# Block-causal attention ahead of two feed-forward layers on one core: every PSUM bank a tile of its own, attention's steps and copies cut by head and bank

## The chip, the cores and the metric

One core of a Trainium2 chip runs the whole program. The metric is device microseconds (us) of one execution, the median of 3 runs. The engines are named as the profile names them: PE is TensorE (PEld its weight load), DVE is VectorE, ACT is ScalarE, POOL is GpSimd, SP is SyncE, which here only starts DMAs. PSUM is the memory that TensorE writes; it has 8 banks of 512 fp32 for each of 128 partitions, and in this kernel DVE and ACT read the products from it.

## The reference, cut to what matters

```python
# q, k, v: (4, 8, 576, 64) fp32; x: 2304 tokens x 512; both layers 512 -> 2048 -> 512
scores = scale * np.matmul(q, k.transpose(0, 1, 3, 2))
mask = (pos[:, None] // 64) >= (pos[None, :] // 64)
scores = np.where(mask, scores, -1e9)
scores = scores - np.max(scores, axis=-1, keepdims=True)
attn = np.exp(scores)
attn = attn / (np.sum(attn, axis=-1, keepdims=True) + 1e-9)
x = np.matmul(attn, v)            # heads side by side: 2304 x 512
h = x @ w_in;  x = np.maximum(h, 0) ** 2 @ w_out
h = x @ w_in2; y = (h * np.cos(h)) @ w_out2
```

## The kernel before

The 32 heads of 576 tokens are taken as 16 pairs (p = 0 to 15), two heads (e = 0, 1) in each. Queries come in five row blocks: m = 0 to 3 of 128 queries each, which see 128(m+1) keys, and the last 64 queries, which see all 576. The last queries of two neighbouring pairs (Q = p // 2) share one step, since 2 x 64 queries fill the 128 partitions. `attention()` does all of it before `layers()` does the two feed-forward layers, whose matmuls (lines 727 and 794) split each fp32 factor into a high and a low half.

For each pair there are these steps, and the line that the profile shows for each:

- **load** (395, 396, 413): keys `kB`, queries `qB` and values `vB` by DMA; **k scale** (400) on GpSimd. Pair 0's keys and queries come in two parts, 256 and 320 keys.
- **scores** (427): a matmul for each head and half block into `ps`. One PSUM tile is a double, `[128, 2, 512]`: head 0 in its first bank, head 1 in its second. There are four doubles.
- **maximum** (475, DVE) and **exponential** (481, ACT, with the row sums in `sums`): one for each head, from PSUM into `P`.
- **last** (454, then 475 and 481 as well): the last 64 queries of two pairs, into two doubles; head e takes one double, the two halves of the keys its two banks. One maximum and one exponential over all 576 keys for each head, into `PL`.
- **guard** (502, GpSimd, adds 1e-9), **invert** (507, DVE), **scale** (519 GpSimd, 517 ACT): divides the rows.
- **turn** (558) and **turn last** (583): transposes of 128x128 on TensorE into a double, both heads in one step. **turned** (564) and **turned last** (597): copies from the double to `PT`, both heads in one instruction of up to 768 elements, on ACT or DVE.
- **weighted** (616): `PT` times values, into one bank, `holds=1`; two for each pair, the first 256 queries and the other 320. **keep** (625) copies that bank to `xall`.

The order is not written out. Every step is added to a `Plan` with its engine, an assumed cost, its reads and writes, the number of banks that it holds and a rank (`RANK`, three numbers for each kind of step). `Plan.emit` then walks a clock of its own over the engines, takes at each turn the step that can start first (of those the one of lowest rank), chooses its banks (`room`) and emits it. Each engine runs its instructions in the order of emission. The waits between engines come from the framework, which looks at the accesses to a tile: one that follows another engine's in the order of emission waits for it. It does so by tile, and a double is one tile.

`weights`, `shift`, `mask` and their like (257 to 310) prepare the layers' weights; `cut` (351, 354) splits `xall` for the first layer. Both begin inside attention.

Of the kernel before, what the change touches and what calls it, by code (L numbers as in the profile page):

```python
# [28 lines left out]
    "load": (-1070.1, 12335.9, 3315.9),  # L29
    "k scale": (4499.4, 4439.0, 10407.1),  # L30
    "scores": (-3717.3, -3706.2, -4224.4),
    "maximum": (-4123.2, -5928.6, -2791.5),
    "exponential": (-2882.2, -4488.5, -2823.0),
    "last": (-4277.4, 3387.7, 5215.9),
    "maximum last": (4504.6, -3957.5, 2890.3),
    "exponential last": (5026.5, 8137.9, 3199.7),
    "guard": (-7573.3, 98.1, 5585.7),
    "invert": (-370.9, -1350.6, 1118.4),
    "scale": (8255.0, 13810.4, 13542.6),
    "guard last": (11229.8, 12038.7, 351.1),  # L40
    "invert last": (-2810.2, -7044.6, -10537.8),
    "scale last": (-6927.0, -1451.2, -1971.5),
    "turn": (9961.4, 12162.8, 5856.4),
    "turned": (-8239.7, -3277.3, -4164.1),
    "turn last": (-7032.9, -15612.2, -19327.9),
    "turned last": (1967.2, -1490.1, -1385.7),
    "value load": (-254.9, -122.1, 2369.7),
    "weighted": (9996.3, 12685.1, 17820.3),
    "keep": (11719.5, 11790.9, 1623.7),
    "weights": (12395.5, 9732.3, 12201.5),  # L50
# [4 lines left out]
class Plan:  # L55
# [8 lines left out]
    STAY = 0.087  # L64

    def __init__(self, doubles):
        self.doubles = doubles
        self.steps, self.wrote, self.readers = [], {}, {}
        self.taken, self.due = {}, {}
# [22 lines left out]
    def bank(self, n, x=0):  # L92
        b = self.taken[n][x]
        return self.doubles[b // 2][:, b % 2]

    def double(self, n, x=0):
        return self.doubles[self.taken[n][2 * x] // 2]

    def room(self, free, holds, t=None):

        if holds == 1:
            able = [(max(at - (t or 0.0), 0.0) if t is not None else at, b ^ 1 in free, b) for b, at in free.items()]
            if not able:
                return None
            b = min(able)[2]
            return free[b], [b]
        pairs = sorted((max(free[b], free[b + 1]), b) for b in free if not b % 2 and b + 1 in free)
        if 2 * len(pairs) < holds:
            return None
        pairs = pairs[: holds // 2]  # L110
        return pairs[-1][0], [b + x for _, b in pairs for x in range(2)]

    def emit(self):
# [13 lines left out]
        free = {b: 0.0 for b in range(2 * len(self.doubles))}  # L127
# [58 lines left out]
def tile_block_causal_attention__then__two_ffn(  # L186
# [174 lines left out]
    def attention():  # L361
        with ExitStack() as actx:
            ap = actx.enter_context(tc.tile_pool(name="ap", bufs=1))
            ps = actx.enter_context(tc.tile_pool(name="ps", bufs=1, space=PSUM))
            plan = Plan([ps.tile([128, 2, 512], F32, name=f"ps{r}") for r in range(4)])
# [7 lines left out]
            PT = [ap.tile([128, NCH, 2, S], F32, name=f"PT{r}") for r in range(2)]  # L373
# [4 lines left out]
            def small(name, n, r):  # L378
                return ap.tile([128, n], F32, name=f"{name}{r}")

            nmax = [[[small(f"nmax{m}.{e}.", 1, r) for e in range(2)] for m in range(NCH)] for r in range(2)]
            sums = [[small(f"sums{g}.", 2 * len(ms), r) for g, ms in enumerate([*groups, (4,)])] for r in range(2)]
            rinv = [[small(f"rinv{g}.", 2 * len(ms), r) for g, ms in enumerate([*groups, (4,)])] for r in range(2)]

            def add_loads(p):
                r, x = p // 2 % 2, p % 2

                cuts = [0, 4, NB] if p == 0 else [0, NB]
                parts = list(zip(cuts, cuts[1:]))
                other = nc.scalar if p == 0 else nc.sync  # L390
                for n, (b0, b1) in enumerate(parts):
                    keys = [f"{y}{r}.{x}.{z}" for y in "kq" for z in (range(2) if p else (n,))]

                    def load(b0=b0, b1=b1):
                        nc.sync.dma_start(out=kB[r][:, x, b0 * D : b1 * D], in_=kT[p, :, b0 * D : b1 * D])
                        other.dma_start(out=qB[r][:, x, b0:b1], in_=qd[p, :, b0:b1])

                    def scale(b0=b0, b1=b1):
# [6 lines left out]
                        "D", (2.8 if p else 2.9 if n == 0 else 1.2), ("load", 10 * p + n), load, writes=keys  # L405
# [3 lines left out]
                        writes=[y for y in keys if y[0] == "k"],  # L409
# [7 lines left out]
            def add_scores(p, m):  # L417
# [4 lines left out]
                def product():  # L422
                    held = plan.double(s)
                    for e, own in enumerate(heads):
                        for h, half in enumerate(heads):
                            c, w = n - 128 + h * D, n - D + h * D
                            nc.tensor.matmul(  # L427
                                held[half, e, 512 - n : 512 - n + w], lhsT=qB[r][own, x, c // D, e],
                                rhs=kB[r][own, x, 0:w], start=True, stop=True,
                            )  # L430
# [3 lines left out]
                    [f"{y}{r}.{x}.{z}" for y in "kq" for z in range(1 if m < 2 else 2)], [f"S{p}.{m}", f"free{x}.{m}"],  # L434
# [4 lines left out]
                add_softmax(  # L439
                    p, x, m, s, f"S{p}.{m}", rank, g, at,  # L440
                    lambda e: plan.double(s)[:, e, 512 - n : 512],
                    lambda e: P[x][:, p_off[m] + e * n :][:, 0:n], n,
                )

            def add_last(Q):

                r, w = Q % 2, S // 2
                rank = 20 * Q

                def product():  # L450
                    for y in range(2):
                        for e, own in enumerate(heads):
                            for x, half in enumerate(heads):
                                nc.tensor.matmul(
                                    plan.double(s, e)[half, y, 0:w], lhsT=qB[r][own, x, NB - 1, e],
# [3 lines left out]
                keys = [f"{a}{r}.{x}.{z}" for a in "qk" for x in range(2) for z in range(2)]  # L459
                s = plan.add(  # L460
                    "P", 4 * S / 2400, ("last", rank), product, keys, [f"SL{Q}", f"free{r}.L"],
                    holds=4, mode="quarters", late=0.4,
                )
                add_softmax(
                    Q, r, NCH - 1, s, f"SL{Q}", rank, len(groups), 0,
                    lambda e: plan.double(s, e)[:, :, 0:w],
                    lambda e: PL[r][:, e, 0:S].rearrange("p (y w) -> p y w", y=2), S,
                )

            def add_softmax(p, r, m, s, at, rank, g, c, held, mine, n):  # L470
                one = m < NM
                name = m if one else "L"

                def maximum(e):
                    nc.vector.tensor_reduce(
                        out=nmax[r][m][e], in_=held(e), axis=AX.X if one else AX.XY,
                        op=ALU.max, negate=True,
                    )

                def exponential(e):  # L480
                    nc.scalar.activation(  # L481
                        out=mine(e), in_=held(e), func=AF.Exp, bias=nmax[r][m][e], scale=1.0,
                        accum_out=sums[r][g][:, c + e : c + e + 1],
                    )

                for e in range(2):
                    kind = "" if one else " last"
                    plan.add(
# [466 lines left out]
```

## Time and profile before

| | us |
|---|---|
| median of 3 runs | 971.17 (971.08 to 974.04) |
| profiled execution, its own time | 970.63 |
| its span in the profile | 968.8 |
| attention, first 20 | PE busy 15.24, DVE 11.30, ACT 13.13, POOL 8.65 |
| attention, 20 to 170 | PE busy 135.98, DVE 116.55, ACT 104.80, POOL 86.91 |
| layers, 170 to 968 | PE busy 792.10, DVE 455.83, ACT 418.37 |

Some 1.8 us of the profiled execution's time lie outside of its span. Busy time is that of an engine's own instructions; what an engine waits for stands in the views of waits and in the brackets of a timeline.

### The profile page before, as it was taken

The page shows a single profiled execution, that of the slowest core. Times are in us where ns is not written, and L with a number is a line of the kernel's source. Part 1 is how long each engine was busy: PE and PEld are TensorE (multiplying, and loading weights), DVE is VectorE, ACT ScalarE, POOL GpSimd, SP SyncE. Part 2 cuts the span into 40 slices and gives each one's busy share as a digit, 9 for nine tenths or more (in the row PEclk, how much of TensorE's full clock was granted, in tenths as well). Part 3 has the DMA queues.
Part 4 walks back from the last instruction along what each step waited for, and adds up shares of the span by engine and source line. Part 5 has one row for each costly group of instructions (what it writes and reads, how often), then busy time and mean ns, then how long its engine had stood idle before and what let it go on. Part 6 is the DMA issues. An engine that isn't in the chain of part 4 may idle for free.

```text
span 968.8 us, 13920 instructions
## 1 busy us (share of the span) xinstructions
PE 943.3 (97%) x5247; PEld 774.6 (80%) x5247; DVE 583.7 (60%) x1148; ACT 536.3 (55%) x1080; POOL 95.6 (10%) x212
## 2 busy tenths in 40 slices
PE   7989899999999999999999999999999999999998
PEld 4666666888888888888888878888888888899996
DVE  6777787777774112111479989565556656556554
ACT  7766668888775334433579975343334434434433
POOL 5666653000000000000000000000000000000000
PEclk9999999999999999999999999999999999999999
DMA  7443411333330000000135530001000100100000
GB/s 269 145 151 102 150 31 49 132 131 131 131 124 30 1 1 1 0 1 1 44 111 181 181 108 8 1 1 44 0 1 1 44 1 1 44 0 1 33 1 33
DMA packets 18947, 58.56 MB, mean 60 GB/s; under 512 B 1984, under 2 KB 2240, under 8 KB 18880
## 3 DMA queue, kind: packets, MB, share of 16 engines
q1 hardware_dynamic: 18592, 57.09, 17.0%
q8 instruction: 41, 0.67, 0.3%
q10 hardware_dynamic: 288, 0.59, 0.2%
q14 instruction: 26, 0.21, 0.1%
HBM read 52.95 MB, written 4.72 MB: 60 GB/s over the span
## 4 chain that ended last, share of the span: by engine, by line
PE 86%; DVE 8%; ACT 5%; issue 1%; ACTq 0%; DVEq 0%
PE h L727 37%; PE acc L794 35%; PE ps L616 5%; PE ps L558 3%; PE ps L427 2%; ACT P L481 2%; PE h L794 2%; DVE w L309 1%; DVE bits L285 1%; DVE raw L279 1%; PE ps L583 1%; DVE xs L354 1%; DVE bits L268 1%; DVE raw L291 1%; ACT bits L274 1%
## 5 line engine op out<-in xcount | busy, mean ns | idle before, releaser
L727 PE MATMUL h<-xs,w 128*128 128x512 f32 (+2 forms) x1920 | 419.5, 369 | 2.2 <-DVE xall L625 0.7
L727 PEld LDWEIGHTS h<-xs,w 128*128 128x128 f32 x1920 | 344.6, 188 | 59.0 <-DVE xs L354 1.0
L794 PE MATMUL acc<-w,gs 128*128 128x512 f32 x864 | 209.9, 391 | 0.2 <-ACT xall L807 0.2
L742 DVE TENSOR_TENSOR gs<-g,gs 128x512 fp32r<-128x512 f32 (+2 forms) x160 | 101.5, 634 | 147.2 <-ACT gs L739 147.1
L794 PEld LDWEIGHTS acc<-w,gs 128*128 128x128 f32 x864 | 161.7, 188 | 32.9 <-ACT xall L807 0.6
L794 PE MATMUL acc<-gs,w 128*128 128x512 f32 x768 | 184.9, 390 | 0.0
L739 ACT CAST gs<-g 128x512 fp32r<-128x512 f32 (+2 forms) x160 | 92.6, 579 | 150.7 <-DVE g L776 100.9
L794 PEld LDWEIGHTS acc<-gs,w 128*128 128x128 f32 x768 | 143.3, 188 | 29.0
L762 DVE SCALAR_TENSOR_TENSOR g<-turns,h 128x512 f32<-128x512 int32 (+1 forms) x80 | 50.7, 634 | 130.6 <-ACT turns L759 130.6
L759 ACT ACTIVATE turns<-h 128x512 int32<-128x512 f32 (+1 forms) x80 | 44.2, 553 | 75.3 <-PE h L727 75.2
L773 ACT ACTIVATE g<-g,half_pi 128x512 f32<-128x512 f32 (+1 forms) x80 | 54.6, 682 | 37.6 <-DVE g L767 37.6
L749 ACT ACTIVATE g<-h 128x512 f32<-128x512 f32 x80 | 43.7, 547 | 55.1 <-PE h L727 55.1
L616 PE MATMUL ps<-PT,vB 128*64 128x320 f32 (+4 forms) x448 | 48.4, 362 | 11.1 <-ACT P L481 7.8
L616 PEld LDWEIGHTS ps<-PT,vB 128*64 128x64 f32 x448 | 29.0, 137 | 33.7 <-ACT P L481 13.7
L306 ACT CAST w<-bits 128x512 fp32r<-128x512 f32 x64 | 39.7, 621 | 27.5 <-DVE bits L285 23.1
L309 DVE SCALAR_TENSOR_TENSOR w<-raw 128x512 fp32r<-128x512 uint32 x64 | 44.3, 693 | 11.2 <-PE h L727 6.7
L776 DVE TENSOR_TENSOR g<-h,g 128x512 f32<-128x512 f32 (+1 forms) x80 | 50.4, 631 | 0.3 <-ACT g L773 0.3
L762 DVE SCALAR_TENSOR_TENSOR g<-turns,g 128x512 f32<-128x512 int32 (+1 forms) x80 | 50.3, 629 | 0.0
L750 ACT ACTIVATE g<-g 128x512 f32<-128x512 f32 x80 | 47.2, 590 | 2.5
L274 ACT ACTIVATE bits<-bits,new_bias 128x512 int32<-128x512 int32 x64 | 46.3, 723 | 0.3 <-DVE bits L268 0.3
L427 PE MATMUL ps<-kB,qB 64*64 64x128 f32 (+7 forms) x512 | 42.6, 433 | 2.6 <-ACT PL L481 1.0
L261 ACT ACTIVATE raw<-raw 128x512 uint32<-128x512 uint32 x64 | 43.4, 679 | 2.8 <-DMA raw<-in_w_dram 2.4
(136 smaller groups left out, 809.5 us busy)
## 6 DMA issues: line engine op xcount, KB each, us to landing
raw<-in_w_dram SPq DMA_DIRECT2D x64, 512.0 KB, 3.6
qB<-in_qd_dram SPq DMA_DIRECT2D x15, 576.0 KB, 4.0
vB<-in_vp_dram SPq DMA_DIRECT2D x16, 320.0 KB, 2.9
kB<-in_kT_dram SPq DMA_DIRECT2D x15, 288.0 KB, 2.8
out_dram<-o SPq DMA_DIRECT2D x8, 512.0 KB, 2.8
out_dram<-o SPq DMA_DIRECT2D x2, 256.0 KB, 2.9
qB<-in_qd_dram ACTq DMA_DIRECT2D x1, 320.0 KB, 5.5
qB<-in_qd_dram ACTq DMA_DIRECT2D x1, 256.0 KB, 2.7
```

Of the source, the lines that this page charges most:

```text
L274: nc.scalar.activation(out=self.bits, in_=self.bits, func=AF.Relu, bias=new_bias, scale=8.0)
L309: nc.vector.scalar_tensor_tensor(out=self.room()[:, 1], in0=self.low_word.bitcast(U32), scalar=2.0**-43, in1=self.high_word.bitcast(F32), ...
L427: nc.tensor.matmul(held[half, e, 512 - n : 512 - n + w], lhsT=qB[r][own, x, c // D, e], rhs=kB[r][own, x, 0:w], start=True, stop=True,)
L616: nc.tensor.matmul(plan.bank(s)[own, a - c0 : c1 - c0], lhsT=vB[x][:, j, e], rhs=PT[x][:, j, e, a:c1], start=(n == 0), stop=(n == len(todo ...
L727: nc.tensor.matmul(h, lhsT=w[:, a, kk * 128 : (kk + 1) * 128], rhs=xs[kk].parts[:, x], start=(m == 0), stop=(m == 3 * KD - 1),)
L739: nc.scalar.copy(out=gs[:, 0], in_=g)
L742: nc.vector.tensor_tensor(out=gs[:, 1], in0=g, in1=gs[:, 0].bitcast(F32), op=ALU.subtract)
L750: nc.scalar.activation(out=g, in_=g, func=AF.Square)
L762: nc.vector.scalar_tensor_tensor(out=g, in0=turns, scalar=-part, in1=start, op0=ALU.mult, op1=ALU.add)
L773: nc.scalar.activation(out=g, in_=g, func=AF.Sin, bias=half_pi, scale=-1.0)
L776: nc.vector.tensor_tensor(out=g, in0=h, in1=g, op=ALU.mult)
L794: nc.tensor.matmul(dst, lhsT=lhsT, rhs=rhs, start=(c == 0 and m == 0 and a % shared == 0), stop=(c == KF - 1 and m == 2 and a % shared == ...
```

## The change

Eight PSUM tiles of one bank take the place of four doubles, and `Plan` hands out single banks: `double` and the part of `room` that looks for pairs of banks go. The steps follow this cut.

- `scores` keeps both heads in one step, but they go to any two banks. Maxima and exponentials are as before, each from a tile of its own.
- `last` becomes two steps, one for each half of the keys (288), each with two banks. Four maxima of 288 take the place of two of 576; a new step `lesser` takes the smaller of two negated maxima (one element); four exponentials of 288 take the place of two of 576, with partial sums in `psum`. `guard last` adds the two partial sums and 1e-9 in one instruction, on DVE instead of GpSimd.
- `turn` and `turn last` become a step for each head with one bank, and `turned` one copy for each head and bank: 384 or 256 elements instead of 768 or 512. `turned last` copies one head for both pairs (before: both heads for one pair), so its four copies stay four, of the same sizes. `PT` becomes one tile.
- Pair 0's keys and queries are loaded in three parts (128, 128 and 320 keys), issued ahead of the plan. Pair 1's load now stands behind a GpSimd memset of one column of its own keys, which follows pair 0's key scaling.
- `RANK` has new numbers, and `STAY` goes from 0.087 to 0, so the order of all steps is another.

```diff
-            plan = Plan([ps.tile([128, 2, 512], F32, name=f"ps{r}") for r in range(4)])
+            plan = Plan([ps.tile([128, 512], F32, name=f"ps{r}") for r in range(8)])
...
-                cuts = [0, 4, NB] if p == 0 else [0, NB]
+            PARTS = [0, 2, 4, NB]
...
+                        if p == 1:
+                            nc.gpsimd.memset(kB[r][:, x, 0:1], 0.0)
+                        if p:
+                            load(p, b0, b1, nc.sync)
...
+                    def lesser(e=e):
+                        nc.vector.tensor_tensor(
+                            out=least[r][:, e : e + 1], in0=part[r][:, e, 0:1], in1=part[r][:, e, 1:2], op=ALU.min
+                        )
...
+                    if last:
+                        nc.vector.scalar_tensor_tensor(
+                            out=total, in0=psum[r][:, 0], scalar=1e-9, in1=psum[r][:, 1], op0=ALU.add, op1=ALU.add
+                        )
+                        return
...
-                def turned(engine):
-                    held = plan.double(s)[:, :, 0 : w // 2].rearrange("p e (n q) -> p e n q", n=n)
-                    copies[engine](out=into(x, kind), in_=held)
+                    def turned(engine, e=e):
+                        held = plan.bank(steps[e])[:, 0:w].rearrange("p (n q) -> p n q", n=n)
+                        copies[engine](out=into(x, kind, e), in_=held)
...
-    "scores": (-3717.3, -3706.2, -4224.4),
+    "scores": (-861.7, -2863.8, -5239.0),
```

ScalarE, the first eight exponentials (pair 0, m = 0 to 3, heads 0 and 1), before. `ps_83` to `ps_86` are the four doubles; what an instruction waits for stands in brackets.

```order
L481 ACTIVATE P_95,sums0.0_121<-ps_83,nmax0.0.0_101 128x128 [waits DVE_49,PE_49]
L481 ACTIVATE P_95,sums0.0_121<-ps_83,nmax0.1.0_102 128x128
L481 ACTIVATE P_95,sums0.0_121<-ps_84,nmax1.0.0_103 128x256 [waits DVE_49,PE_49]
L481 ACTIVATE P_95,sums0.0_121<-ps_84,nmax1.1.0_104 128x256
L481 ACTIVATE P_95,sums1.0_122<-ps_85,nmax2.0.0_105 128x384 [waits DVE_49,PE_49]
L481 ACTIVATE P_95,sums1.0_122<-ps_85,nmax2.1.0_106 128x384
```

The same after; `ps_83` to `ps_90` are now the eight banks.

```order
L448 ACTIVATE P_99,sums0.0_118<-ps_83,nmax0.0_104 128x128 [waits DVE_49]
L448 ACTIVATE P_99,sums0.0_118<-ps_84,nmax0.0_104 128x128 [waits DVE_49]
L448 ACTIVATE P_99,sums0.0_118<-ps_85,nmax1.0_105 128x256 [waits DVE_49]
L448 ACTIVATE P_99,sums0.0_118<-ps_86,nmax1.0_105 128x256 [waits DVE_49]
L448 ACTIVATE P_99,sums1.0_119<-ps_87,nmax2.0_106 128x384 [waits DVE_49]
L448 ACTIVATE P_99,sums1.0_119<-ps_88,nmax2.0_106 128x384 [waits DVE_49]
```

Before, only the first head's exponential waits, once for both heads; after, each waits for its own maximum.

TensorE in the middle of attention, from a pair's scores of m = 2 to a weighted product, before:

```order
L427 MATMUL ps_84<-kB_91,qB_89 64x320
L427 MATMUL ps_84<-kB_91,qB_89 64x384
L427 MATMUL ps_84<-kB_91,qB_89 64x320
L427 MATMUL ps_84<-kB_91,qB_89 64x384
L427 MATMUL ps_85<-kB_91,qB_89 64x448
L427 MATMUL ps_85<-kB_91,qB_89 64x512
L427 MATMUL ps_85<-kB_91,qB_89 64x448
L427 MATMUL ps_85<-kB_91,qB_89 64x512
L558 MATMUL ps_83<-ident,P_96 128x128 x6
L558 MATMUL ps_86<-ident,P_96 128x128 x4
L616 MATMUL ps_84<-PT_99,vB_93 64x320 x6
```

Such a place after, with the last queries' two steps (line 475) between the scores and the weighted product:

```order
L427 MATMUL ps_85<-kB_95,qB_93 64x384
L427 MATMUL ps_88<-kB_95,qB_93 64x320
L427 MATMUL ps_88<-kB_95,qB_93 64x384
L427 MATMUL ps_83<-kB_95,qB_93 64x448
L427 MATMUL ps_83<-kB_95,qB_93 64x512
L427 MATMUL ps_86<-kB_95,qB_93 64x448
L427 MATMUL ps_86<-kB_95,qB_93 64x512
L475 MATMUL ps_89<-kB_96,qB_94 64x288 x2
L475 MATMUL ps_90<-kB_96,qB_94 64x288 x2
L475 MATMUL ps_84<-kB_96,qB_94 64x288 x2
L475 MATMUL ps_87<-kB_96,qB_94 64x288 x2
L643 MATMUL ps_85<-PT,vB_97 64x320 x6
```

In both the weighted product writes a bank that held the m = 2 scores of head 0. Before, that bank's tile also held head 1's scores; after, they stand in `ps_88`.

GpSimd, from the first key scaling to the first scaling of rows, after (before, the keys of pair 1 were scaled behind one guard, and no memset stood there):

```order
L400 TENSOR_SCALAR kB_95<-kB_95 128x128 [waits DMAHW1_49]
L400 TENSOR_SCALAR kB_95<-kB_95 128x128 [waits DMAHW3_49]
L400 TENSOR_SCALAR kB_95<-kB_95 128x320 [waits DMAHW5_49]
L394 MEMSET kB_95 128x1
L530 TENSOR_SCALAR sums0.0_118<-sums0.0_118 128x4 [waits Activation_49]
L530 TENSOR_SCALAR sums1.0_119<-sums1.0_119 128x2 [waits Activation_49]
L400 TENSOR_SCALAR kB_95<-kB_95 128x576 [waits DMAHW7_49,Pool_49]
L547 TENSOR_SCALAR P_99<-P_99,rinv0.0_126 128x128 [waits DVE_49]
```

SP's load of pair 1 waits for that memset, and the loads of the pairs after it are behind pair 1's on SP.

## Rows read from the trace of the kernel before

**Rows 1.** Busy time by stretch: start:end, length, then each engine's busy time (instructions), granted clock, DMA share, GB/s.

```profile
0.00:20.00 20.00, 15.24 (x127) 9.37 (x131) 11.30 (x35) 13.13 (x40) 8.65 (x25) 0.91 0.81 293
20.00:170.00 150.00, 135.98 (x1380) 93.17 (x1374) 116.55 (x270) 104.80 (x319) 86.91 (x188) 1.00 0.32 107
170.00:968.00 798.00, 792.10 (x3744) 672.06 (x3744) 455.83 (x845) 418.37 (x723) 0.00 (x0) 1.00 0.13 46
```

**Rows 2.** PE's waits, 0 to 172: line, releaser, us in total, times, longest.

```profile
PE ps L616 <- ACT P L481: 7.8, 12, 1.3
PE ps L558 <- ACT P L481: 2.1, 4, 1.3
PE ps L616 <- DVE xall L625: 2.1, 4, 0.5
```

**Rows 3.** Timeline around 56 to 60: start, duration, engine, line; in brackets idle before.

```profile
56.35 2.38 PE L427 MATMUL ps<-kB,qB 64*64 64x320 f32 x32
...
57.35 0.56 DVE L475 TENSOR_REDUCE nmax2.0.1_115<-ps 128x1 f32<-128x384 f32 x1
57.82 0.55 DVE L475 TENSOR_REDUCE nmax2.1.1_116<-ps 128x1 f32<-128x384 f32 x1
...
58.49 0.58 ACT L481 ACTIVATE P<-ps,nmax2.0.1_115 128x384 f32<-128x384 f32 x1 [2.06 <-DVE nmax2.1.1_116 L475]
...
59.06 0.57 ACT L481 ACTIVATE P<-ps,nmax2.1.1_116 128x384 f32<-128x384 f32 x1
...
59.77 0.76 PE L616 MATMUL ps<-PT,vB 128*64 128x320 f32 x4 [1.04 <-ACT P L481]
```

**Rows 4.** Timeline of PE around 35 to 39 and at 110, then of DVE around 38.

```profile
34.84 2.92 PE L616 MATMUL ps<-PT,vB 128*64 128x256 f32 x28 [0.32 <-ACT P L481]
38.29 0.87 PE L616 MATMUL ps<-PT,vB 128*64 128x256 f32 x8 [0.53 <-DVE xall L625]
...
109.59 3.50 PE L558 MATMUL ps<-ident,P 128*128 128x128 f32 x30
...
37.81 0.43 DVE L625 COPY xall<-ps 128x256 f32<-128x256 f32 x1 [1.33 <-PE ps L616]
```

**Rows 5.** Opening: timeline of ACT, of PE, then busy time by stretch (as Rows 1).

```profile
6.10 0.37 ACT L481 ACTIVATE P<-ps,nmax0.0.0_101 128x128 f32<-128x128 f32 x1 [3.88 <-DVE nmax0.1.0_102 L475]
...
7.22 0.47 ACT L481 ACTIVATE P<-ps,nmax1.0.0_103 128x256 f32<-128x256 f32 x1 [0.31 <-DVE nmax1.1.0_104 L475]
...
8.98 0.58 ACT L481 ACTIVATE P<-ps,nmax2.0.0_105 128x384 f32<-128x384 f32 x1 [0.74 <-DVE nmax2.1.0_106 L475]
...
10.85 0.68 ACT L481 ACTIVATE P<-ps,nmax3.1.0_108 128x512 f32<-128x512 f32 x1
...
13.29 3.27 PE L427 MATMUL ps<-kB,qB 64*64 64x320 f32 x16 [0.96 <-ACT PL L481]
16.49 1.36 PE L558 MATMUL ps<-ident,P 128*128 128x128 f32 x10
...
14.00:16.00 2.00, 2.00 (x16) 0.70 (x8) 1.02 (x2) 1.57 (x6) 1.77 (x5) 0.50 0.92 365
```

**Rows 6.** Groups by line and shape, 0 to 172: count, then busy us, mean ns.

```profile
L564 DVE COPY PT<-ps 128x768 f32<-128x768 f32 x25 | 23.6, 953 | 6.2 <-PE ps L558 6.2
L597 DVE COPY PT<-ps 128x384 f32<-128x384 f32 x6 | 3.3, 555 | 0.4 <-PE ps L583 0.4
L597 ACT COPY PT<-ps 128x384 f32<-128x384 f32 x10 | 4.6, 479 | 7.7 <-DVE PT L597 7.7
L475 DVE TENSOR_REDUCE nmax4.0.0_109<-ps 128x1 f32<-128x576 f32 x4 | 3.0, 744 | 0.0
L481 ACT ACTIVATE PL<-ps,nmax4.0.0_109 128x576 f32<-128x576 f32 x4 | 3.1, 764 | 0.0
```

**Rows 7.** Line 354 (two SBUF operands) by shape, 0 to 172, then 175 to 969.

```profile
L354 DVE TENSOR_TENSOR xs<-xall,xs 128x512 fp32r<-128x512 f32 x4 | 4.0, 993 | 0.7 <-ACT xs L351 0.7
L354 DVE TENSOR_TENSOR xs<-xall,xs 128x512 fp32r<-128x512 f32 x24 | 15.5, 689 | 13.4 <-ACT xs L351 13.3
```

More of the change, by code (lines that the diff above doesn't have):

```diff
@@ L92, in bank @@
     def bank(self, n, x=0):
[L93 to L97, printed above, removed]
+        return self.banks[self.taken[n][x]]
     def room(self, free, holds, t=None):
[L101 to L108, printed above, removed]
-            return None
-        pairs = pairs[: holds // 2]
-        return pairs[-1][0], [b + x for _, b in pairs for x in range(2)]
+        first = sorted((at if t is None else max(at - t, 0.0), b) for b, at in free.items())[:holds]
+        if len(first) < holds:
+            return None
+        return max(free[b] for _, b in first), [b for _, b in first]
     def emit(self):
@@ L126, in emit @@
                     able[engine].append(n)
-        free = {b: 0.0 for b in range(2 * len(self.doubles))}
+        free = {b: 0.0 for b in range(len(self.banks))}
         due, idle = dict(self.due), {}
@@ L408, in add_loads @@
                         "G", 0.16 + (b1 - b0) * 0.055, ("k scale", 10 * p + n), scale,
[L409 removed]
+                        writes=[y for y in keys if y[0] == "k"] + (["scaled"] if p == 0 else []),
                     )
@@ L454, in product @@
                                 nc.tensor.matmul(
-                                    plan.double(s, e)[half, y, 0:w], lhsT=qB[r][own, x, NB - 1, e],
+                                    plan.bank(steps[y], e)[half, 0:w], lhsT=qB[r][own, x, NB - 1, e],
                                     rhs=kB[r][own, x, y * w : (y + 1) * w], start=True, stop=True,
                                 )
[L459 to L477, printed above, removed]
-                    )
[L480 to L488, printed above, removed]
-                        "V", 0.066 + n / 960, ("maximum" + kind, rank + e / 2), lambda e=e: maximum(e), [at],
-                        [f"nmax{r}.{name}.{e}"],
-                    )
-                    plan.add(
-                        "A", 0.23 + n * 0.000875, ("exponential" + kind, rank + e / 2), lambda e=e: exponential(e),
-                        [at, f"nmax{r}.{name}.{e}"], [f"P{r}.{name}.{e}", f"sum{r}.{name}.{e}"],
-                        frees=(s, (e,) if one else (2 * e, 2 * e + 1)),
-                    )
@@ L509, in add_normalise @@
                 names = [f"{m}.{e}" for m in ms for e in range(2)]
-                keys = [f"sum{r}.{name}" for name in names]
-                plan.add("G", 0.28, ("guard" + last, rank), guard, writes=keys)
+                keys = [f"sum{r}.{name}{y}" for name in names for y in ((".0", ".1") if last else ("",))]
+                plan.add("V" if last else "G", 0.1 if last else 0.28, ("guard" + last, rank), guard, writes=keys)
                 plan.add("V", 0.1, ("invert" + last, rank), invert, keys, [f"rinv{r}.{g}"])
@@ new lines, in add_turns @@
+                    mine = [f"P{x}.{m}.{e}" for m in ms] + [f"free{x}.{m}" for m in ms]
+                    if not e:
+                        steps = []
+                    steps.append(plan.add(
+                        "P", 0.109 * n, ("turn", rank + e / 2), product, mine, [f"T{p}.{kind}.{e}", f"room{x}.{kind}.{e}"],
+                        holds=1, mode="all",
+                    ))
+                    plan.add(
+                        "AV", (0.06 + w / 1200, 0.066 + w / 960), ("turned", rank + e / 2), turned, [f"T{p}.{kind}.{e}"],
+                        [f"PT{x}.{kind}.{e}"], frees=(steps[e], (0,)),
+                    )
@@ L585, in product, with turned @@
                                 PL[r][:, e, 128 * j : 128 * j + 128], ident,
                             )
[L588 to L600 removed]
+                    def turned(engine, e=e):
+                        held = plan.bank(steps[e])[:, 0:w].rearrange("p (j x q) -> p x j q", x=2, q=D)
+                        copies[engine](out=PT[:, :, j0:j1, e, S - D : S], in_=held)
```

224 lines of the change are left out of this document (132 added, 92 removed).

## The prediction, made before the changed kernel ran

> **What bounds the kernel now.** I read the busy time by stretch first [rows 1]. From 170 us on TensorE is busy 792.1 of 798 us: the layers are bound by it, the change does not touch them, and they only start earlier or later. So the change is worth what it does to the first 170 us. There, from 20 to 170, TensorE is busy 136.0 of 150 us, DVE 116.6, ACT 104.8 and POOL 86.9; in the first 20 it is busy 15.2. No other engine is full, so the 14 + 4.8 us that TensorE is idle are latency: it waits for something that comes back late. That is the ceiling, some 18.8 us.
>
> The waits of TensorE say for what [rows 2]. The largest, 7.8 us in 12 pieces, is the weighted product (line 616) held by an exponential (481). It does not read what that exponential writes; it needs the PSUM that the exponential empties. The next are transposes held the same way, 2.1 us, and weighted products held by a copy to `xall` (625), 2.1 us.
>
> The third view is a timeline of one such wait [rows 3]. The products of 56.35 end at 58.73 (start and duration). DVE's maximum of head 0 ends at 57.91, that of head 1 at 58.37, and only then, at 58.49, does ACT begin head 0's exponential: it waited 2.06 us and was released by head 1's maximum, a value that it does not use. Then head 1's exponential ends at 59.63, and the weighted product, which overwrites head 0's bank only, starts at 59.77, 1.04 us after TensorE was free. Both detours come from the double being one tile: the wait is for its last user, in whichever bank.
>
> **Part 1: exponential to weighted product.** With a tile for each bank, head 0's exponential needs head 0's maximum alone: 57.91 plus the 0.12 between release and start seen above (58.37 to 58.49) is 58.03; it takes 0.58, so ends at 58.61; plus the 0.14 seen above (59.63 to 59.77) the bank is free at 58.75. TensorE was free at 58.73. Of 1.04 us, 0.02 stay: the detour costs about 1.0 us, as long as almost the longest of the 12 waits (1.3). In the old order nearly all of the 7.8 us would go. But the order is another. The ordered rows show 16 to 20 score or last matmuls in a row and then 14 or 18 weighted ones, into banks whose exponentials stand early among those of the run. I walk one such run of 20, with the bank of m = 1, head 0, wanted next: DVE still has two copies of the transposes ahead (0.7, my estimate) and three short instructions (0.3), its first maximum of 128 is done at 1.3; ACT starts 0.12 later, takes 0.37 twice and 0.47 once (128, 128, 256) [rows 5], so the bank is free at 2.6 + 0.14 = 2.75. TensorE takes 2.38 for 16 products [rows 3], some 2.5 for 20: 0.25 us are left. I add 0.1 for the second weighted run: 0.35 for a round of two pairs. One of the 12 waits (0.4) belongs to the opening, so 7.4 us of them are in the steady part; seven rounds keep 7 x 0.35 = 2.5. **Gain 4.9 us**, between 1 (new waits as long as half a detour in every round) and 7.4.
>
> **Part 2: weighted product to weighted product.** The product of 34.84 is two in a row, and a third follows at 38.29 after 0.53 us [rows 4]. The third needs the first one's bank. Its copy takes 0.43 us and was idle 1.33 us before it: it began at 37.81, at the end of the second product (34.84 + 2.92 = 37.76), because that went to the other bank of the same tile. With own tiles the copy runs beneath the second product. All four waits of 0.53, **gain 2.1 us**; 1.1 if half of them come back as waits for the copy itself in DVE's queue.
>
> **Part 3: transposes behind exponentials.** The 2.1 us [rows 2] shrink in the same way, to about 0.5: **gain 1.6**, between 0 and 2.1.
>
> **Part 4: the opening.** ACT's first eight exponentials start at 6.10 and end at 11.53 (10.85 + 0.68) with 0.31 and 0.74 us of waits for a second head's maximum among them, so 4.4 us of work [rows 5]. After, the first needs neither the second head's products nor its maximum, about 0.2 each: it starts near 5.7 and the eight end near 10.1. By the ordered rows four scalings of `P` follow on ACT (some 0.5 each, like exponentials of their widths) and two exponentials of 128 (0.37), then the first 20 transposes can start: near 12.8. Before, they start at 16.49. But the new order puts eight products behind them that stood ahead: the 3.27 us at 13.29, which ran in a stretch with a granted clock of 0.50, so about 1.6 at full clock. 16.49 - 12.8 - 1.6 = 2.1; **gain 2.0 us**. The ends: 0 if the clock falls for longer than before (below), 3.5 if it does not fall. TensorE was busy 15.2 of the first 20 us [rows 1] and the granted clock fell to 0.50, that is 1.2 GHz, from 14 to 16 after waits of 0.9 us and more; the new opening waits no less before 12.8, so I leave the clock's price as it is.
>
> Pair 1's loads now leave SP only after three key scalings and a memset on GpSimd, and GpSimd scales pair 1's keys ahead of its first row scaling. I cost this at nothing: the first row scaling waits for the guards anyway, and a guard waits for exponentials that end near 8 us. If pair 1 lands after 9.5 us instead, every microsecond later moves the whole opening.
>
> **Part 5: the extra instructions.** 64 copies of 768 or 512 become 128 of 384 or 256; by the ordered rows DVE gets 29 and ACT 35 of the 64 more. A copy of 768 takes 0.953 us on DVE, one of 384 0.555 [rows 6]; neighbours overlap by about 0.09 (the two maxima of [rows 3] start 0.47 apart and take 0.56), so two copies cost 1.02 for 0.95, +0.07. I take the same on ACT, whose copy of 384 is 0.479: 64 x 0.07 = 4.5 us over both engines. A maximum of 576 takes 0.744, one of 384 0.555, so one of 288 about 0.46: two cost 0.74 for 0.65, +0.09, 16 times; an exponential of 576 takes 0.764, one of 384 0.58, so 288 about 0.49 and +0.22 for each of 16, 3.5 us on ACT [rows 3, 6]. The 16 `lesser` and 8 `guard last` are new on DVE and no row shows them: below, 0.1 us each like a short instruction without a wait; above, what [rows 7] show of another DVE instruction with two SBUF operands. It takes 0.993 us in attention, where GpSimd works, and 0.689 later, where GpSimd has nothing [rows 1, 7]: 0.30 us more, 24 x 0.30 = 7.3. All told DVE gets 5 to 13 us more and ACT some 6. Over 150 us that is 122 to 130 and 111, still below TensorE's 136, so most hides beneath TensorE. The cover is thin where transposes run: thirty take 3.50 us [rows 4], so forty in a row take 4.7, and they bring 16 copies. **I charge 1.0 us**, 0 at best and 6 if half of the extra work on both engines lies on the path.
>
> The Trainium skill has a rule that speaks against this part: by SBUF — State Buffer, section "SBUF: two separate sides", a VectorE instruction with two SBUF inputs and a GpSimd instruction that reads SBUF share ports under an exclusive lock, and the one that comes second waits out the whole of the other. The trace agrees in kind (0.993 against 0.689). By that rule each of the 24 would wait for up to a whole GpSimd instruction.
>
> **The sum.** -4.9 - 2.1 - 1.6 - 2.0 + 1.0 = -9.6 us against the profiled execution's own 970.63, 1.8 of which lie outside its span of 968.8; that is 961.0. The median shown is 971.17, 0.54 above it, so I forecast **961.6**.
>
> **Rivals.** (a) *Everything goes*: all of parts 1 to 3 (7.4 + 2.1 + 2.1) and 3.5 in the opening, at no charge: 15.1, so 956.1. For it: the worked example leaves 0.02. Against: the new order packs TensorE's runs tighter, which shortens the time in which banks come free.
>
> (b) *The gain is eaten by the split work.* Parts 1 to 3 give only 1 + 1.1 + 0, the opening 2, and the extra work costs 3 to 4: 970 to 971, no change. For it: DVE is busy 78% already. Against: it has 33 us of slack, and it is not the engine that the waits name for its work, but for the tile.
>
> (c) *VectorE paces the transposes, slower.* Forty transposes (4.7 us) bring 16 copies, four maxima of `last` and two `lesser`. If DVE takes ten copies (4.0 us at about 0.4), the maxima (1.5) and two `lesser` that each lose 0.7 beside GpSimd, it needs 6.9 us for the 4.7: 2.2 us for each round, 15 over seven, which less 9.6 of gain makes some 977. It decides from 1.4 us a round on. By the Trainium skill's page named above this is what the lock does. Against it: by the ordered rows ACT and DVE share those copies about equally, which gives DVE some 5 us.
>
> (d) *The opening goes wrong*: pair 1 late, or the clock at 0.50 for 6 us instead of about 3. Part 4 is then -1.5 to +1 instead of -2: 962 to 965, still faster.
>
> **Chances.** The forecast (957 to 966) 0.58, (a) 0.09, (d) 0.10, (b) 0.16, (c) 0.07. Within 0.3%, 2.9 us, is about what a measurement of this kernel can tell from no change: faster means under 968.3. (b) gives a quarter of its chance to faster: 0.81; same 0.12; slower 0.07. The range leaves out most of (c) and the far ends of (a) and (b): 955.5 to 969.5.
>
> **What would show it.** Right: exponentials of head 0 released by head 0's maximum; TensorE's waits for line 481's successor below 4 us in all and none of 0.53 behind `xall`; the first transposes near 12.8; attention's end near 161; the layers as long as before. Wrong: TensorE's idle time in attention still above 15 us, under other names: copies in the runs of transposes, `lesser` long beside GpSimd, or pair 1's keys scaled after 9.5 us.

## The result, and the profile after

The changed kernel takes **957.16 us** (median of 4, 956.83 to 958.58) against 971.12 beside it: ratio 0.9852, 95% interval 0.9831 to 0.9874, so 14.0 us less. The profiled execution has a span of 955.0 us. The forecast of 961.6 was 4.4 us too high; the range held it, and rival (a), 956.1, came nearest.

First the start of the layers in the timeline of the kernel before, then its busy time up to there by stretch (columns as in [rows 1], which were cut at 170).

```profile
170.28 4.46 PE L727 MATMUL h<-xs,w 128*128 128x512 f32 x24 [0.66 <-DVE xall L625]
175.22 0.96 PE L727 MATMUL h<-xs,w 128*128 128x512 f32 x3 [0.48 <-ACT g L749]
```

```profile
0.00:170.28 170.28, 151.22 (x1503) 102.54 (x1503) 128.13 (x305) 118.21 (x359) 95.56 (x212) 0.99 0.38 128
```

The same two views of the changed kernel:

```profile
154.64 4.45 PE L756 MATMUL h<-xs,w 128*128 128x512 f32 x24
160.75 4.46 PE L756 MATMUL h<-xs,w 128*128 128x512 f32 x24 [1.66 <-ACT g L778]
```

```profile
0.00:154.64 154.64, 146.36 (x1503) 104.83 (x1503) 130.89 (x377) 126.20 (x427) 92.91 (x202) 1.00 0.41 138
20.00:157.00 137.00, 134.21 (x1382) 97.41 (x1379) 120.34 (x338) 114.75 (x388) 84.61 (x177) 1.00 0.36 121
14.00:16.00 2.00, 1.29 (x9) 0.84 (x9) 2.00 (x6) 1.92 (x10) 0.67 (x1) 1.00 0.98 383
```

Attention ends 15.64 us earlier (170.28 to 154.64). TensorE's idle time ahead of that point falls from 170.28 - 151.22 = 19.06 to 8.28, its busy time from 151.22 to 146.36, with 1503 instructions in both. From there to the end of the span the layers take 800.36 us instead of 798.52: 1.84 us are given back, which leaves 13.8. DVE and ACT do 2.8 and 8.0 us more in a shorter time. Between 20 and 157 TensorE is busy 134.2 of 137 us: by its busy time, attention is now bound by it.

What TensorE still waits for from 0 to 160 (columns as in [rows 2]):

```profile
PE ps L475 <- ACT P L448: 1.7, 1, 1.7
PE ps L427 <- POOL kB L394: 1.4, 1, 1.4
...
PE ps L588 <- ACT PL L510: 0.8, 1, 0.8
PE ps L588 <- ACT P L448: 0.7, 2, 0.5
PE ps L643 <- DVE PT L622: 0.7, 1, 0.7
```

Line 643 (616 before) waits neither for an exponential (448, 481 before) nor for a copy to `xall` (652, 625 before); the 7.8 and 2.1 us of [rows 2] are gone. Both waits at the head of this list belong to the opening (the one left out, 1.4, stands ahead of the first product, before as after).

One round, timeline (answers to [rows 3, 4]):

```profile
65.84 4.72 PE L588 MATMUL ps<-ident,P 128*128 128x128 f32 x40
...
70.49 2.60 PE L427 MATMUL ps<-kB,qB 64*64 64x64 f32 x40
...
72.47 0.47 ACT L448 ACTIVATE P<-ps,nmax1.1_109 128x256 f32<-128x256 f32 x1
73.09 0.76 PE L643 MATMUL ps<-PT,vB 128*64 128x256 f32 x6
```

The products of 70.49 write the bank of m = 1, head 0. Its exponential is the one of 72.47, which ends at 72.94; with the 0.14 of [rows 3] the bank is free at 73.08, and the weighted product starts in it at 73.09, as TensorE comes free. Forty transposes run in 4.72 us without a wait.

The opening, timeline (answers to [rows 5]):

```profile
5.81 0.37 ACT L448 ACTIVATE P<-ps,nmax0.0_104 128x128 f32<-128x128 f32 x1 [2.17 <-DVE nmax0.0_104 L442]
7.17 0.46 POOL L400 TENSOR_SCALAR kB<-kB 128x320 f32<-128x320 f32 x1 [3.27 <-DMA kB<-in_kT_dram]
7.69 1.73 PE L427 MATMUL ps<-kB,qB 64*64 64x320 f32 x16 [1.38 <-POOL kB L394]
9.18 0.58 ACT L448 ACTIVATE P<-ps,nmax2.0_106 128x384 f32<-128x384 f32 x1 [1.36 <-DVE nmax2.0_106 L442]
...
10.97 0.69 ACT L448 ACTIVATE P<-ps,nmax3.0_107 128x512 f32<-128x512 f32 x1
...
14.34 0.74 PE L588 MATMUL ps<-ident,P 128*128 128x128 f32 x5 [0.52 <-ACT P L448]
...
19.05 0.87 PE L643 MATMUL ps<-PT,vB 128*64 128x256 f32 x8
```

Head 0's exponential is released by head 0's maximum, as forecast. But the third part of pair 0's keys lands only shortly before 7.17, and ACT waits 1.36 us ahead of m = 2, so the eight exponentials end at 11.66 (10.97 + 0.69) and not near 10.1. Transposes start at 14.34, not 12.8.

The new shapes (groups, answers to [rows 6, 7]):

```profile
L594 DVE COPY PT<-ps 128x384 f32<-128x384 f32 x42 | 22.7, 552 | 2.5 <-PE ps L588 1.6 <-ACT PT L594 0.3
L510 ACT ACTIVATE PL<-ps,least 128x288 f32<-128x288 f32 x32 | 16.3, 517 | 1.3 <-DVE least L499 1.3
L499 DVE TENSOR_TENSOR least<-part 128x1 f32<-128x1 f32 x16 | 3.4, 217 | 0.0
```

### The profile page after: what moved, and what is told of

The parts are those of the page before. It is cut to its first block, busy times and chain, and to the rows that moved or that the text cites. A ratio compares the mean times of both kernels' runs of the same rounds, so it can differ in the third digit from the quotient of the medians.

```text
span 955.0 us, 14053 instructions
## 1 busy us (share of the span) xinstructions
PE 938.5 (98%) x5247; PEld 776.5 (81%) x5247; DVE 586.4 (61%) x1221; ACT 545.2 (57%) x1151; POOL 92.9 (10%) x202
## 3 DMA queue, kind: packets, MB, share of 16 engines
HBM read 52.95 MB, written 4.72 MB: 60 GB/s over the span
## 4 chain that ended last, share of the span: by engine, by line
PE 85%; DVE 8%; ACT 2%; DMA 2%; POOL 1%; issue 1%; SPq 0%; DVEq 0%; ACTq 0%; POOLq 0%
PE h L756 36%; PE acc L823 35%; PE ps L643 4%; PE ps L588 3%; PE ps L427 3%; PE h L823 2%; DVE w L299 1%; DVE bits L275 1%; DVE raw L269 1%; DMA kB<-in_kT_dram 1%; DVE bits L258 1%; PE ps L615 1%; DVE raw L281 1%; DVE gs L771 1%; POOL P L547 1%
## 5 line engine op out<-in xcount | busy, mean ns | idle before, releaser
L275 DVE SCALAR_TENSOR_TENSOR bits<-raw,bits 128x512 int32<-128x512 int32 x64 | 44.0, 687 | 0.9 <-ACT bits L264 0.9
```

The lines of the kernel that those rows point to most:

```text
L275: nc.vector.scalar_tensor_tensor(out=self.bits, in0=self.high_word, scalar=-(2**31), in1=self.bits, op0=ALU.bitwise_and, op1=ALU.bitwise_or,)
```

## The experiments

Two theories stood against each other. T1: the gain is that a bank is a tile of its own, so that nothing waits for the user of another bank. T2: it is the new order and the opening. Kernels whose label begins with a are the changed kernel with one edit, those with b the kernel before with one.

### Tiles, split work and order

**b_own_tiles**: the order and loads of before, eight tiles, each instruction that covered two banks split in place.

```diff
-            plan = Plan([ps.tile([128, 2, 512], F32, name=f"ps{r}") for r in range(4)])
+            plan = Plan([ps.tile([128, 512], F32, name=f"ps{r}") for r in range(8)])
...
-                    held = plan.double(s)[:, :, 0 : w // 2].rearrange("p e (n q) -> p e n q", n=n)
-                    copies[engine](out=into(x, kind), in_=held)
+                    for e in range(2):
+                        held = plan.bank(s, e)[:, 0 : w // 2].rearrange("p (n q) -> p n q", n=n)
+                        copies[engine](out=into(x, kind, e), in_=held)
```

> The kernel before, in its own order and with its own opening, with eight tiles of one bank; each instruction that covered two banks is two in the same place (copies, maxima and exponentials of last, a min of the two maxima; the sum's 1e-9 is left out in last). T1: waits by doubles go, 971 less 7.4, 2.1 and 1.6, plus 1 to 3 for the split work: 961 to 964. T2: the order was made for doubles and keeps its waits: 968 to 973.

Measured 956.32 us (955.6 to 958.91), ratio 0.9838 (0.9814 to 0.9862): as fast as the changed kernel. It is T1's direction, but 5 us below T1's range of 961 to 964; T2's 968 to 973 is refuted.

**b_split_doubles**: the same split work in the same order, the banks halves of four tiles again.

```diff
-            plan = Plan([ps.tile([128, 512], F32, name=f"ps{r}") for r in range(8)])
+            two = [ps.tile([128, 2, 512], F32, name=f"ps{r}") for r in range(4)]
+            plan = Plan([held[:, x] for held in two for x in range(2)])
```

> The kernel before in its own order with every instruction over two banks split in two, as in the one with own tiles, but the banks again halves of four tiles of two. It differs from the kernel before by the split work alone, from the one with own tiles by the tiles alone. Theory T1: the waits by doubles stay, and the split work costs what part 5 charged, 0 to 6 us: 971 to 977, and the whole step to 956.3 is the tiles'. T2b (part of the gain of the one with own tiles is the split itself, since a copy of one bank is done earlier): 960 to 969.

Measured 977.44 us (975.71 to 979.18), ratio 1.0075 (1.0058 to 1.0092). TensorE's waits in this kernel, 0 to 178:

```profile
PE ps L635 <- ACT P L495: 9.2, 12, 1.6
PE ps L576 <- ACT P L495: 4.0, 8, 1.4
PE ps L635 <- DVE xall L644: 2.1, 4, 0.5
```

And all that is left of these three kinds in b_own_tiles, 0 to 158 (there 634, 575 and 494):

```profile
PE ps L634 <- ACT P L494: 0.8, 1, 0.8
PE ps L575 <- ACT P L494: 0.5, 1, 0.5
```

The two differ in the tiles alone (`PT` is one tile in both): 977.44 to 956.32, **21.1 us**, and the twelve, eight and four waits become two. They ran on two chips; against the kernel before beside each (970.4 and 971.4) it is 7.0 + 15.1 = 22.1 us. With doubles the split work costs 7.0 us, 0.4 above T1's 971 to 977: TensorE waits longer for ACT's exponentials (9.2 against 7.8, 4.0 against 2.1), which is 3.3 us of it; the rest isn't taken apart. With own tiles that cost can't be seen. T2b, that the split itself gains, falls.

**a_doubles**: the edit of b_split_doubles in the changed kernel.

> The changed kernel, in its own order, with its eight banks as halves of four tiles of two banks. Theory T1 (the gain is that a bank is a tile of its own, so nobody waits for the user of the other bank): waits of line 643 behind line 448 and behind the xall copies come back, and because the plan gives out banks singly they may be more than in the kernel before; 8 to 15 us slower than after, 965 to 972. Theory T2 (the gain is the new order and the opening, the tiles only allow it): within 3 us of after, 955 to 960.

Measured 1037.65 us (1035.18 to 1040.25), ratio 1.067 (1.0638 to 1.0701). Its largest waits, 0 to 235 (lines one higher than in the changed kernel):

```profile
PE ps L644 <- ACT P L449: 8.2, 9, 2.1
PE ps L476 <- DVE nmax3.0_103 L443: 7.9, 4, 2.0
```

The direction was T1's, the size was missed by 66 us (T1 allowed 972 at most): I had counted the old waits. The new plan gives out banks singly, and here a product also waits for maxima (L443), 7.9 us in all, as it nowhere does in the changed kernel. Up to the start of the layers TensorE is idle 62.4 us (8.3 in the changed kernel) and busy 176.4 (146.4), at a mean granted clock of 0.94 instead of 1.00, so not all of the loss is waiting.

**a_numbers_before**: the old `RANK` and `STAY` in the changed kernel.

> The changed kernel with the order's numbers (RANK, STAY) of the kernel before, the number of lesser kept. T1: most of the gain stays, 958 to 962. T2: most of it goes, 965 to 971.

Measured 974.31 us (972.56 to 976.54), ratio 1.0029 (1.0014 to 1.0044). T1's 958 to 962 is refuted, and T2's 965 to 971 is exceeded by 3 us. TensorE's two largest waits, 0 to 175:

```profile
PE ps L588 <- ACT P L448: 4.5, 11, 1.1
PE ps L588 <- ACT PL L510: 2.9, 1, 2.9
```

The old numbers give another order here than in the kernel before, since the steps are cut otherwise: now transposes wait for exponentials, eleven times for those of the row blocks, once 2.9 us for one of `last`. Up to the start of the layers TensorE is idle 8.4 us more than in the changed kernel and busy 10.9 more (157.27), with a granted clock of 0.66 from 150 to 160; that busy time isn't explained here. So order counts, 17 us of it, but the new order is not what gained: the old one, kept step by step, does as well (b_own_tiles). New numbers were needed because the steps were cut by head and bank.

### The opening

**a_open_before**: before's loads in the changed kernel and its order (two parts, pair 1 right behind, no memset), ahead of the plan.

```diff
-                        if p == 1:
-                            nc.gpsimd.memset(kB[r][:, x, 0:1], 0.0)
-                        if p:
+                        if p > 1:
                             load(p, b0, b1, nc.sync)
...
-            for b0, b1 in zip(PARTS, PARTS[1:]):
+            for b0, b1 in ((0, 4), (4, NB)):
                 load(0, b0, b1, nc.scalar)
+            load(1, 0, NB, nc.sync)
```

> The changed kernel in its own order with the loads as before: pair 0 in two parts, pair 1 sent right behind it without the memset. Theory T3 (the opening gives back what part 4 said, 2 us or more, since pair 0 has the DMA for itself): the first transposes later than 14.34 by 1 us or more, the clock perhaps at 0.50 again, 959 to 962. Rival: the third part's landing at 7.17 and the wait of 1.4 us for it cost as much as the first part gains: 956 to 958, first transposes at 13.8 to 14.5.

Measured **953.45 us** (953.04 to 955.24), ratio 0.9808 (0.9784 to 0.9833), the fastest of all. Both expectations missed, T3 in the sign: three of its four times lie under the lowest of the eight taken of the changed kernel (955.23), the fourth beside it. Timeline:

```profile
4.63 2.73 PE L427 MATMUL ps<-kB,qB 64*64 64x64 f32 x32
9.02 1.06 PE L475 MATMUL ps<-kB,qB 64*64 64x288 f32 x8 [1.66 <-ACT P L448]
...
12.16 0.74 PE L588 MATMUL ps<-ident,P 128*128 128x128 f32 x5 [0.94 <-ACT P L448]
...
16.49 0.87 PE L643 MATMUL ps<-PT,vB 128*64 128x256 f32 x8
```

All products of pair 0 run in one go from 4.63; in the changed kernel those of m = 2 begin at 7.69. The first transposes are 2.2 us earlier, the first weighted products 2.6. Up to 0.7 us of that can belong to this execution and not to the loads: the first sixteen products took 1.56 or 0.88 us in kernels that open alike (last section).

**a_three_ungated** (three parts, pair 1 right behind, no memset) and **a_two_gated** (two parts, with the memset), each one half of that edit:

> The changed kernel with pair 0 in three parts as changed, and pair 1's loads sent right behind them, without the memset. Theory G (what the new opening costs is that pair 1 waits for pair 0's third scaling): near the kernel with before's loads, 953 to 955, first transposes near 12.2. Theory H (it is the three parts: smaller pieces land later, so the products of m=2 and m=3 wait): 956 to 959, products of m=2 still not before 7.5.

> The changed kernel with pair 0 in two parts and pair 1 still behind the memset. G: 956 to 958, the last products after 10.5. H: 953 to 955, products of m=2 and m=3 straight behind those of m=0 and m=1, before 6.5.

Measured 956.98 (956.33 to 957.99; ratio 0.9854, 0.9839 to 0.987) and 956.16 (954.64 to 956.51; 0.9842, 0.9826 to 0.9858). Of the first, then of the second:

```profile
7.29 2.85 PE L425 MATMUL ps<-kB,qB 64*64 64x320 f32 x16 [1.82 <-DMA qB<-in_qd_dram]
```

```profile
9.65 0.70 PE L477 MATMUL ps<-kB,qB 64*64 64x288 f32 x2 [1.86 <-ACT P L450]
10.54 0.47 PE L477 MATMUL ps<-kB,qB 64*64 64x288 f32 x3 [0.19 <-DMA qB<-in_qd_dram]
...
12.90 0.74 PE L590 MATMUL ps<-ident,P 128*128 128x128 f32 x5 [0.52 <-ACT P L450]
```

With three parts m = 2 waits whether pair 1 is held back or not, as H says (at 7.29, a little ahead of H's 7.5). With two parts it does not, and pair 1 behind the memset costs TensorE a wait of 0.19 us. Transposes come at 12.90 instead of 12.16, but 0.63 us of that is there when the last products begin (9.65 against 9.02), ahead of any use of pair 1. The first time is H's and the second G's, so neither theory holds alone. By the times neither half alone is to be told from the changed kernel (955.23 to 958.62 in eight); only both together give the 3 us. In one profile of each, the two parts bring more: attention ends at 152.72 with them alone, at 151.85 with both, at 154.64 in the changed kernel. How the two share the gain stays open.

**a_open_late**: a_open_before with the loads behind ACT's first instruction.

> The changed kernel with before's loads (two parts, pair 1 at once), but written behind the first ACT instruction as in the kernel before, so that ACT loads its table ahead of pair 0's query loads. If the place of the loads matters, queries land later by about the table load, 1.28 us: first transposes near 13.4 and 954.5 to 956. If not, as with the loads ahead, 952.5 to 954.5.

Measured 955.77 (954.98 to 957.18; ratio 0.9844, 0.9827 to 0.986). The time is that of the case that the place matters, and by the trace the first transposes (13.07) and the first weighted product (17.40 against 16.49) come 0.9 us later. But the queries do not land later, as that case had it. ACT's queue starts its two query loads at 0.91, beside the table load of 0.73 to 2.01 and not behind it (0.73 in a_open_before), and they take 2.9 and 4.2 us to land against 3.5 and 4.3. What is longer is TensorE's run of pair 0's products:

```profile
4.75 3.46 PE L427 MATMUL ps<-kB,qB 64*64 64x64 f32 x32
```

It takes 3.46 us against 2.73, a difference that the first sixteen products alone can make from one execution to the next (last section). Whether the place of the loads matters stays open.

**b_own_early**: b_own_tiles with the loads of pairs 0 and 1 written first.

> The kernel before in its own order with eight tiles of one bank, with its loads of pairs 0 and 1 written ahead of everything, ACT's table load too. If the wait of 1.6 us for queries and the stretch with the clock at 0.50 were due to the late queries: 952 to 954. If the order of that kernel brings the low clock whatever the loads do: 955 to 957.

Measured 955.72 (955.63 to 956.38; ratio 0.9842, 0.9827 to 0.9856): within the spread of b_own_tiles. Its profile has no low clock and the first transposes at 13.80 against 17.04, but the profile of b_own_tiles was of its slowest execution (958.91, mean granted clock 0.997; 955.6 and 955.69 at 1.000). The gain of 2 us or more that the first case promised isn't there.

### The extra work

**after_beside** is the changed kernel on the same chip as the next two.

> The changed kernel itself, as the measure beside the other three on this chip: 956 to 958.5, and in executions with a mean granted clock under 0.998 one to two us more than in those above it.

Measured 956.22 (955.23 to 958.62; ratio 0.986, 0.9841 to 0.9879). Three executions at a mean granted clock of 0.998 and 0.999 took 955.23 to 956.64, the one at 0.996 took 958.62: 2.0 to 3.4 us more, where one to two were expected.

**a_more_splits**: each copy of transposed blocks in two.

```diff
-                        copies[engine](out=into(x, kind, e), in_=held)
+                        copies[engine](out=into(x, kind, e)[:, 0:1], in_=held[:, 0:1])
+                        copies[engine](out=into(x, kind, e)[:, 1:n], in_=held[:, 1:n])
```

> The changed kernel with each copy of transposed blocks in two on the same engine: 128 copies more, by the 0.07 us of part 5 some 9 us over both engines. Cover theory (DVE and ACT have room beneath TensorE): within 1.5 us of the changed kernel, 956 to 958.5. Rival: the room is used up, copies pace the runs of forty transposes: 960 to 966.

Measured 959.1 (958.41 to 961.65; ratio 0.989, 0.9871 to 0.9909): 2.9 us slower, between the two. Runs of forty transposes in after_beside, then here:

```profile
29.31 4.71 PE L588 MATMUL ps<-ident,P 128*128 128x128 f32 x40
...
65.56 4.72 PE L588 MATMUL ps<-ident,P 128*128 128x128 f32 x40
...
117.20 4.85 PE L588 MATMUL ps<-ident,P 128*128 128x128 f32 x40
```

```profile
30.71 4.79 PE L588 MATMUL ps<-ident,P 128*128 128x128 f32 x40
...
67.52 4.92 PE L588 MATMUL ps<-ident,P 128*128 128x128 f32 x40
...
120.16 4.79 PE L588 MATMUL ps<-ident,P 128*128 128x128 f32 x40
```

Between the first and the last of these lie five rounds: 87.89 us become 89.45, 1.6 us more or some 0.3 a round, by pieces too short to be listed as waits. Another 1.4 us of the profiled loss was there before the first of them, where this execution had a granted clock of 0.50 from 12 to 14 and after_beside's had 1.00. At like clocks the loss stays (958.41 at 0.999 here, 955.23 and 955.8 there). That the added copies pace TensorE is the likely cause, but no wait names them.

**a_more_lesser**: each `lesser` four times.

```diff
                     def lesser(e=e):
-                        nc.vector.tensor_tensor(
+                        for _ in range(4):
+                            nc.vector.tensor_tensor(
```

> The changed kernel with each min of two maxima done four times, 48 short DVE instructions with two SBUF operands more; at the 0.217 us of the row 10.4 us on DVE, which stand in the path from maximum to exponential of last. Cover theory: up to 2 us slower, 957 to 959. Rival (each is held up beside GpSimd as the first one was, 0.63): 20 us on DVE, 963 or more.

Measured 970.76 (968.5 to 975.37; ratio 1.0009, 0.9996 to 1.0023): 14.5 us slower, the whole gain of the change. Timeline, GpSimd beside DVE:

```profile
74.47 0.59 POOL L548 TENSOR_SCALAR P<-P,rinv1.0_127 128x384 f32<-128x384 f32 x1
74.54 0.53 DVE L500 TENSOR_TENSOR least<-part 128x1 f32<-128x1 f32 x1
75.04 0.70 POOL L548 TENSOR_SCALAR P<-P,rinv2.0_128 128x512 f32<-128x512 f32 x1
75.11 0.63 DVE L500 TENSOR_TENSOR least<-part 128x1 f32<-128x1 f32 x1
...
76.33 0.55 DVE L595 COPY PT<-ps 128x384 f32<-128x384 f32 x1
76.93 0.77 PE L589 MATMUL ps<-ident,P 128*128 128x128 f32 x5 [1.54 <-DVE PT L595]
```

Groups of these mins and of the exponentials that need them, 0 to 170:

```profile
L500 DVE TENSOR_TENSOR least<-part 128x1 f32<-128x1 f32 x64 | 16.9, 266 | 1.7
L511 ACT ACTIVATE PL<-ps,least 128x288 f32<-128x288 f32 x32 | 16.1, 509 | 8.5 <-DVE least L500 8.4
```

Each of the two mins of one element in the timeline ends when the GpSimd scaling beside it ends: 75.07 and 75.06, then 75.74 and 75.74. The copy behind them starts at 76.33, and the run of transposes stops for 1.54 us. The rule of the Trainium skill that the prediction named (SBUF — State Buffer, "SBUF: two separate sides": whichever of the two starts first keeps the shared ports for its whole instruction) is seen here at work. The mean of the 64 is 266 ns, far from 0.63. In all they take 16.9 us of DVE, 13.5 more than in the changed kernel, and ACT's exponentials of `last` wait 8.4 us for them instead of 1.3. At the median of 0.16 us the 48 added ones would come to 7.7 us (my estimate), so some 6 of the 13.5 are time beside GpSimd; how much of the loss is that, and how much the plain length of the string, no run separates. Up to the start of the layers TensorE is idle 8.2 us longer than in after_beside and busy 6.5 us longer, and three stretches around 14, 35 and 58 us have a granted clock of 0.50, the last two behind stops of 2.27 and 1.90 us; after_beside's profile has none. So a part of the 14.5 us is the clock's. The rival had the time right (963 or more), not the reason (0.63 for each).

## Why the prediction held, and where it was 4.4 us too high

**What bounds the kernel**: right. TensorE was held by users of the other half of a tile. The pair b_split_doubles and b_own_tiles shows it at one order.

**Part 1**, 4.9 forecast, between 1 and 7.4: all of it went, 7.8 in the waits, 7.4 of that in the steady part. The step that failed is "0.25 us are left": bank free 2.75 us after the run's start, TensorE done after 2.5. Measured 2.59 and 2.60. Both guesses of the walk were off by a tenth or two, and 0.35 in each of seven rounds, 2.5 us, hung on that. A difference so small between two estimates should have been taken as nothing, with 2.5 in the range alone.

**Part 2**, 2.1: all gone, as forecast. **Part 3**, 1.6: the waits of transposes behind exponentials go from 2.1 to 1.5 (0.8 and 0.7): a gain of 0.6, the term was a microsecond too large. That the idle time as a whole fell by 10.8, where parts 1 to 4 make 10.6, is partly luck: part 1 was too small by 2.5, part 3 too large by 1.0, and the opening gained otherwise than forecast.

**Part 4**, 2.0: the first weighted product comes 1.8 us earlier (19.05 against 20.87 in the trace before), but not by the steps named. Transposes at 14.34 instead of 12.8, because of a landing that the prediction did not cost: a_two_gated, with pair 0 in two parts, has them at 12.90. Instead the granted clock stayed at 1.00 from 14 to 16, where [rows 5] show 0.50. The loads in three parts and the memset, taken for harmless, cost some 3 us together (957.16 or 956.22 against 953.45). Of the two the prediction watched only pair 1 ("after 9.5 us": it was scaled at 10.77); the part that came late first was pair 0's third.

**Part 5**, +1.0: TensorE's waits name nothing of it, and b_own_tiles, which has it, is no slower. The 64 extra copies went 33 to DVE and 31 to ACT, not 29 and 35; all told DVE did 2.8 us more, not 5 to 13, and ACT 8.0, not 6. The direction of the doubt was right: with 128 copies more the cost is 2.9, with 48 mins more 14.5 (the clock's share included), with tiles of two banks 7.0, 1 over the upper bound of 6. Rival (c) did not come true: in the run of transposes at 65.84 the two mins take 0.32 and 0.17, where it had each lose 0.7. In a_more_lesser, with four in a row, the same mechanism stops such a run.

**Not in the sum**: TensorE's busy time fell by 4.9 us. The 13 to 18 us of the profile before at a clock of 0.50 to 0.84 account for at most 1.7 of it (1 us at 0.61, 2 at 0.50, 2 at 0.84); the rest, with the same number of instructions in fewer, longer runs, stays open. The tiles alone don't bring it: b_own_tiles is busy 151.00 with a like low stretch, b_own_early 148.68 without one. So attention's end, forecast near 161, came at 154.64. And the layers, forecast "as long as before", give back 1.84: their first product no longer waits 0.66 for attention's last copy, but the next waits 1.66 for ACT instead of 0.48 and a later one 1.3 instead of 0.5, since ACT had not got further. A start that only one engine can use earlier isn't a gain.

Together, over the profiled spans: -10.8 of idle time, -4.9 of busy time, +1.8 in the layers, -13.8, where the forecast had -9.6.

## What to carry to other kernels

When an engine waits for a buffer, look at which part of it the releaser used: here eight tiles for four, with the order untouched, were worth 21 us at the same split work, and 15 us against the kernel before, whose instructions were not split. Numbers that set an order belong to the steps they were made for, so cut steps and order change together or not at all. Loads in smaller parts, and the next load held back for them, are to be tried alone: here the two together cost some 3 us of what the tiles gained, and the changed kernel with the old loads is the version to keep (953.45).

## What was not expected of the hardware

The same program has executions with different mean granted clocks: the changed kernel took 956.83 at 1.000, 956.91 at 0.998, 957.41 at 0.997 and 958.58 at 0.996. So the absence of the low stretch in the one profile after can be a trait of that execution, and isn't shown to be one of the change. Nor does a lower mean always go with a longer time: a_three_ungated took 956.89 at 0.995 and 956.33 to 957.99 at 1.000.

The first sixteen products differ in the same way. They take 1.56 us in the profiles of the kernel before, the changed kernel and after_beside, but 0.88 in a_more_splits and 1.19 in a_more_lesser, which open as the changed kernel does. The granted clock reads 1.00 there in all five; why they differ isn't shown.

A load with less traffic beside it did not land earlier: pair 0's last 160 KB of keys took 5.4 us to land in the changed kernel, where DMA share had fallen to 0.15 between 6 and 7 us, and 3.7 us with the old loads, where all of pair 1 followed. Why isn't settled here; a_three_ungated, with three parts and pair 1 behind, took 4.6 us and had its last keys scaled at 6.33.
